# Attention, then two expert layers: another order of steps in a pair's turn, and copies dealt to other engines

## The chip, the cores and the metric

The kernel runs on one core of one Trainium2 chip. The metric is the device time of one execution in microseconds (us). The core has five engines, each with its own queue that it takes in order: TensorE (PE in the profile, its weight loads PEld), VectorE (DVE), ScalarE (ACT), GpSimd (POOL) and SyncE (SP, which here only issues transfers).

## What is computed

Causal attention with decay over 4 batches of 8 heads, 576 rows, head size 64; its output goes as 2304 rows of 512 through two expert layers of 8 experts each. The change is in the attention:

```python
scores = scale * np.matmul(q, k.transpose(0, 1, 3, 2))
cum = np.cumsum(np.log(np.clip(f, 0.0001, 1.0)), axis=-1)
decay = cum[:, :, :, None] - cum[:, :, None, :]
scores = np.where(causal, -1000000000.0, scores + decay)
attn = np.exp(scores - np.max(scores, axis=-1, keepdims=True))
attn = attn / (np.sum(attn, axis=-1, keepdims=True) + 1e-09)
out = np.matmul(attn, v)
```

The first expert layer picks one expert per row by the largest of 8 logits and weights its output with the softmax value and a second gate; the second layer gives each expert at most 288 rows in the order of the logits.

## The kernel before, in words

**Turns.** `attention` (L542) goes over 16 pairs of heads, 4 per batch, and four more turns to empty its pipeline. In turn i five generators, each a stage of another pair, are stepped one after the other; a step runs to the generator's next `yield`, and what it issues goes to the queues of its engines at once. So the order in which steps are called is the order in each engine's queue. The stages are

- **c**, `causal` (L141), for the pair of turn i+1: on POOL, the decay rows of one pair are copied with the causal mask filled in (L150, four selects of growing width, two per step), then for the last 64 rows two more selects and two copies of q into a block-diagonal tile (L156, L158). Three steps.
- **s**, `scores` (L161), for pair i: matmuls of q and k into a tile of two PSUM banks (L187; rows 0 and 1, row 2, row 3, and the tail rows, L196, whose weights are the tile that c filled), then on VectorE, per row and head, one operation that adds the mask, scales and takes the row's extreme (L176), and on ScalarE, one row later, the exponential with its sum (L173). Five steps; the last issues only the last exponential.
- **f**, `flip` (L209), for pair i-1: transposes of the exponentials on TensorE into a bank of `ps_t` (L215, L240, L245) and copies out of it into `pt` by `evac` (L203): L207 on ScalarE, L205 on VectorE, by a flag in the call. Seven steps with work: for each of the two heads j the column blocks kb=0 and kb=1 (with the last of kb=3), then kb=2 of both heads, the tail rows' four blocks (z4), and their last 64 columns.
- **v**, `values` (L250), for pair i-2: matmuls of `pt` and v into two banks, oA (columns 0 to 255) and oB (256 to 575), and copies of them into `ot`. Five steps: oA; oB for kb=0, 1, 2; oB for kb=3 and 4 with its copy.
- **r**, `rows` (L271), for pair i-3: small operations on VectorE for the reciprocal sums, then two transposes of `ot` back (L282, L288), each followed by a multiplication on VectorE out of the bank (L283, L289). Three steps with work.
- **g**, `Rt.gate` (L375), from turns 7, 11, 15 and 19 on, for a whole batch: its matmuls L381, transposes L389 and L395, a row of small operations on VectorE, the counting matmuls L421 and L424, and five scatters of rows by indirect transfers on POOL (L452), one per step. Sixteen steps, so it lasts for three turns; the last one runs by itself after the last turn.

**The order.** `ORDER` (L539) is a string written out by hand, one letter per step. After it (L589) the stages that have steps left are stepped in rounds until only g is left; so each turn has one more step of g, and the ends of c and s, behind the string. After each step of the string one small operation of the consts is issued on VectorE (`slow.issue`, L588), while there are any. At the end of a turn SP's queue gets the loads of k, q, the decay rows (cb) and, once per batch, v for the pair of two turns later (L601 to L603), and in turns 1 to 7 the clearing of a buffer (L598).

**Buffers.** PSUM has eight banks: the scores have two tiles of two, `ps_t` has two of one for all transposes of f, r and g in turn (a bank is taken again when the copy or multiplication out of it is done), oA and oB have one each. The masks of c and the tiles of f have two buffers each, loads three.

**After the attention** the last gate runs alone, the counts are ranked on VectorE, the rows are scattered and gathered by transfers, and the expert layers follow, with their weights loaded from the start of that phase.

Of the kernel before, what the change touches and what calls it, by code (L numbers as in the profile page):

```python
# [17 lines left out]
B, H, S, D = 4, 8, 576, 64  # L18
# [4 lines left out]
NQ = 4  # L23
SQ = NQ * 128
TL = S - SQ
NI = NQ + 1
T0 = 128 - TL
# [46 lines left out]
class Attention:  # L74
# [134 lines left out]
    def flip(self, zt, z4):  # L209
        nc = self.nc  # L210
        ptt = self.ptp.tile([128, 2, NQ * S + TL], F32, name="pt")
        pt = ptt[:, :, :NQ * S].rearrange("p j (k q) -> p j k q", k=NQ)

        def tr(o, z, i, kb):
            nc.tensor.transpose(o, z[:, CB0[i] + 128 * kb:CB0[i] + 128 * kb + 128], self.ident)  # L215

        for j in range(2):
            z = zt[j]
            t = self.ps_t.tile([128, 512], F32, name="tp")
            for i in range(NQ):  # L220
                tr(t[:, 128 * i:128 * i + 128], z, i, 0)
            self.evac(pt[:, j, 0, :SQ], t, j == 0)
            yield
            t = self.ps_t.tile([128, 512], F32, name="tp")
            for i in range(1, NQ):
                tr(t[:, 128 * i:128 * i + 128], z, i, 1)
            tr(t[:, 0:128], z, 3, 3)
            self.evac(pt[:, j, 1, 128:SQ], t[:, 128:SQ])
            self.evac(pt[:, j, 3, 384:SQ], t[:, 0:128])
            yield  # L230
        t = self.ps_t.tile([128, 512], F32, name="tp")
        for j in range(2):
            for i in range(2, NQ):
                o = 256 * j + 128 * (i - 2)
                tr(t[:, o:o + 128], zt[j], i, 2)
        self.evac(pt[:, :, 2, 256:SQ], t.rearrange("p (j q) -> p j q", j=2), True)
        yield
        t = self.ps_t.tile([128, 512], F32, name="tp")
        for kb in range(NQ):
            nc.tensor.transpose(t[:, 128 * kb:128 * kb + 128], z4[:, 128 * kb:128 * kb + 128], self.ident)  # L240
        self.evac(pt[:, :, :NQ, SQ:S].rearrange("p j k q -> p k j q"),
                  t.rearrange("p (k j q) -> p k j q", k=NQ, j=2))
        yield
        t = self.ps_t.tile([128, 512], F32, name="tp")
        nc.tensor.transpose(t[:, :128], z4[:, S - 128:S], self.ident)  # L245
        self.evac(ptt[T0:, :, NQ * S:], t[T0:, :128].rearrange("p (j q) -> p j q", j=2))
        yield
        return pt, ptt

    def values(self, pt, ptt, vt):  # L250
        nc = self.nc
        oA = self.ps_o.tile([128, 512], F32, name="oA")
        oB = self.ps_o.tile([128, 512], F32, name="oB")
        ot = self.op.tile([128, S], F32, name="ot")
        for t, q0, q1, kbs in ((oA, 0, 256, (0, 1)), (oB, 256, S, (0, 1, 2, 3, 4))):
            for kb in kbs:
                a = max(q0, 128 * kb)
                k0 = 0 if kb < NQ else T0
                for j in range(2):
                    nc.tensor.matmul(t[64 * j:64 * j + 64, a - q0:q1 - q0],  # L260
                                     lhsT=vt[k0:, kb, 64 * j:64 * j + 64],
                                     rhs=pt[:, j, kb, a:q1] if kb < NQ else ptt[k0:, j, NQ * S:],
                                     start=(kb == 0), stop=(kb == kbs[-1]), skip_group_check=True)
                if q0 and kb < 3:
                    yield
            self.evac(ot[:, q0:q1], t[:, :q1 - q0], q0 > 0)
            if not q0:
                yield
        return ot
# [266 lines left out]
HOLD = 6  # L536
LO = 2
LAST = "oosvsssssssssvss"
ORDER = "sfvgcfsfvgrsfvgcfsfvgrfvgr"  # L539


def attention(A, Rt, slow, weights, more, qT, kT, v):  # L542
# [10 lines left out]
    for i in range(T + 4):  # L553
# [22 lines left out]
        def step(k):  # L576
            if k in live:
                try:
                    next(live[k])
                except StopIteration as e:  # L580
                    del live[k]
                    if k != "g":
                        got[k, i - lag[k]] = e.value

        for k in ORDER:
            step(k)
# [1527 lines left out]
```

## Time and profile before

| what | value |
|---|---|
| median of 3 runs | 784.29 us (783.74 to 787.36) |
| the profiled execution's own time | 783.33 us |
| its span (first to last instruction) | 781.6 us |
| TensorE busy over the span | 707.0 us (90%) |
| VectorE, ScalarE, GpSimd busy | 370.8, 383.0, 483.0 us |
| the turns begin (first scores of turn 0) | 10.0 us |
| the experts begin (first of their transposes) | 240.6 us |

Times of rows are in microseconds from the start of the span, "mean ns" in nanoseconds. The ends of matmuls are modelled, so the distance from one group's start to the next group's start tells more than a group's length. Idle time in square brackets or behind the second bar is that of the engine just before the instruction, with what released it.

### The profile page before, as it was taken

Reading aid. Unit: us, or ns where it says so; the run is one execution under the profiler, and the core shown is the slowest. Engines: PE = TensorE matmul, PEld = TensorE weight load, DVE = VectorE, ACT = ScalarE, POOL = GpSimd, SP = SyncE. Lnnn points to the kernel's source line nnn. Section 1 sums busy time; section 2 is a strip of 40 time slices with the busy share of each in tenths; the row PEclk is TensorE's granted clock in tenths of the full one; section 3 lists DMA queues with packets and bytes.
Section 4 is the critical chain, followed back from the end, with each engine's and each line's share of the span. In section 5 each row is a group of like instructions: output and inputs, shape, how many; then the busy total and the mean of one; then the engine's idle time right before and its main releaser. Section 6 shows DMA issues by size and latency. Waiting matters only on the chain. (4 is left out here: it accounts for less than half of the span.)

```text
span 781.6 us, 16048 instructions
## 1 busy us (share of the span) xinstructions
PE 707.0 (90%) x5691; PEld 569.5 (73%) x5691; DVE 370.8 (47%) x1419; ACT 383.0 (49%) x893; POOL 483.0 (62%) x495
## 2 busy tenths in 40 slices
PE   6999999999816999999999999279999999989993
PEld 3555555555506999999999999168978878788892
DVE  4776686776752221321321323756756665651120
ACT  5777666667304454554555652134435344354440
POOL 6455318243234876777777772259868777698861
PEclk9999999999976999999999999569999999999997
DMA  6587566130138616538438430357536617366201
GB/s 215 173 290 278 167 190 216 63 121 2 42 103 279 211 52 241 184 120 273 161 138 276 156 137 12 84 166 247 193 130 206 216 47 265 113 223 200 101 33 39
DMA packets 79492, 124.33 MB, mean 159 GB/s; under 512 B 11085, under 2 KB 43853, under 8 KB 79392
## 3 DMA queue, kind: packets, MB, share of 16 engines
q1 hardware_dynamic: 73056, 104.06, 40.1%
q0 software_dynamic: 6288, 18.97, 6.7%
q8 instruction: 49, 0.80, 0.4%
q14 instruction: 51, 0.42, 0.2%
q10 hardware_dynamic: 48, 0.07, 0.0%
HBM read 101.08 MB, written 22.71 MB: 158 GB/s over the span
## 5 line engine op out<-in xcount | busy, mean ns | idle before, releaser
L699 POOL TENSOR_TENSOR wl<-wraw,wh 128x1024 fp32r<-128x1024 f32 x128 | 305.1, 2400 | 91.3 <-ACT wh L695 86.2
L729 PE MATMUL ph<-xh,wh 128*128 128x288 f32 (+6 forms) x512 | 160.8, 314 | 0.2 <-ACT xh L1922 0.2
L729 PE MATMUL ph<-xl,wh 128*128 128x288 f32 (+6 forms) x512 | 153.4, 300 | 1.5 <-DVE xl L1916 1.5
L729 PE MATMUL ph<-xh,wl 128*128 128x288 f32 (+6 forms) x512 | 153.0, 299 | 0.0
L695 ACT CAST wh<-wraw 128x1024 fp32r<-128x1024 f32 x128 | 132.0, 1050 | 42.2 <-DMA wraw<-in_moe_w_dram 42.2
L733 DVE SCALAR_TENSOR_TENSOR hl<-ph,hh 128x256 fp32r<-128x256 f32 (+6 forms) x128 | 56.3, 443 | 105.8 <-ACT hh L757 60.1
L173 ACT ACTIVATE z<-z,mx 128x128 f32<-128x128 f32 (+2 forms) x144 | 84.1, 585 | 35.4 <-DVE mx L176 34.7
L729 PEld LDWEIGHTS ph<-xh,wh 128*128 128x128 f32 x512 | 97.3, 190 | 5.2 <-issue 3.4
L757 ACT ACTIVATE hh<-ph 128x256 fp32r<-128x256 f32 (+6 forms) x128 | 51.5, 403 | 100.7 <-PE ph L729 97.1
L729 PEld LDWEIGHTS ph<-xl,wh 128*128 128x128 f32 x512 | 97.3, 190 | 2.4 <-DVE xl L1916 2.1
L729 PEld LDWEIGHTS ph<-xh,wl 128*128 128x128 f32 x512 | 97.2, 190 | 0.2 <-POOL wl L699 0.2
L176 DVE CUSTOM_DVE_ANT_0 z<-ps,cx 128x128 f32<-128x128 f32 (+2 forms) x144 | 68.9, 518 | 38.5 <-PE ps L187 23.8
L729 PE MATMUL ph<-hh,wh 128*128 128x288 f32 (+6 forms) x256 | 79.2, 309 | 0.0
L729 PE MATMUL ph<-hh,wl 128*128 128x288 f32 (+6 forms) x256 | 76.8, 300 | 0.9 <-POOL wl L699 0.8
L729 PE MATMUL ph<-hl,wh 128*128 128x288 f32 (+6 forms) x256 | 76.7, 300 | 0.0
L150 POOL TENSOR_SCALAR_AFFINE_SELECT cx<-cb 128x256 f32<-128x256 f32 (+1 forms) x64 | 44.5, 729 | 47.9 <-DMA cb<-c8d 20.3
L215 PEld LDWEIGHTS tp<-ident,z 128*128 128x128 f32 x320 | 33.6, 141 | 42.2 <-issue 12.3
L452 POOL DMA_INDIRECT xs<-x,idx x20 | 19.9, 995 | 68.2 <-DVE x L448 55.2
L215 PE MATMUL tp<-ident,z 128*128 128x128 f32 x320 | 52.2, 286 | 6.5 <-DVE pt L205 4.3
L207 ACT COPY pt<-tp 128x384 f32<-128x384 f32 (+3 forms) x112 | 43.1, 415 | 25.1 <-PE tp L245 12.4
L793 PE MATMUL ph<-wh,hh 128*128 128x512 f32 x128 | 54.2, 423 | 0.0
L793 PE MATMUL ph<-wh,hl 128*128 128x512 f32 x128 | 50.5, 394 | 0.0
(331 smaller groups left out, 1232.9 us busy)
## 6 DMA issues: line engine op xcount, KB each, us to landing
wraw<-in_moe_w_dram SPq DMA_DIRECT2D x128, 512.0 KB, 6.7
cb<-c8d SPq DMA_DIRECT2D x15, 576.0 KB, 6.1
xs<-zrow SPq DMA_DIRECT2D x8, 803.1 KB
xg<-xs SPq DMA_DIRECT2D x7, 771.0 KB, 4.8
kd<-in_k_dram SPq DMA_DIRECT2D x16, 288.0 KB, 7.7
qd<-in_q_dram SPq DMA_DIRECT2D x16, 288.0 KB, 4.7
vt<-in_v_dram SPq DMA_DIRECT2D x4, 1024.0 KB, 8.1
x<-zrow SPq DMA_DIRECT2D x1, 1080.0 KB
```

The costliest lines, as they stand in the source:

```text
L150: nc.gpsimd.affine_select(cx[:, :, CB0[i]:CB0[i] + w], cb[:, :, :w], pattern=[[0, 2], [-1, w]], compare_op=ALU.is_ge, fill=-8e9, base=128 ...
L173: nc.scalar.activation(z, z, AF.Exp, bias=mx[:, c:c + 1], scale=-1.0, accum_out=sm[:, c:c + 1])
L176: nc.vector.tensor_tensor_reduce(out=z, in0=p, in1=cx, scale=-0.125, scalar=3e38, op0=ALU.add, op1=ALU.min, accum_out=mx[:, c:c + 1])
L207: self.nc.scalar.copy(o, i)
L215: nc.tensor.transpose(o, z[:, CB0[i] + 128 * kb:CB0[i] + 128 * kb + 128], self.ident)
L452: st = nc.gpsimd.indirect_dma_start(out=self.xs[:, :], out_offset=bass.IndirectOffsetOnAxis(ap=idx[:, i:i + 1], axis=0), in_=x[:, i, :], i ...
L695: nc.scalar.copy(wh, t)
L699: nc.gpsimd.tensor_sub(wl[:, q], t[:, q], wh.bitcast(F32)[:, q])
L729: mm = lambda o, w, m, st, sp: nc.tensor.matmul(o, lhsT=w, rhs=m, start=st, stop=sp)
L733: nc.vector.scalar_tensor_tensor(out=hl[:, :W], in0=p[:, :W], scalar=0.0, in1=hh.bitcast(F32)[:, :W], op0=ALU.max, op1=ALU.subtract)
L757: nc.scalar.activation(hh[:, :W], p[:, :W], AF.Relu)
L793: mm = lambda o, w, m, st, sp: nc.tensor.matmul(o, lhsT=w, rhs=m, start=st, stop=sp)
```

## The change

The copies' engines come from a table (1 is VectorE, 0 ScalarE), and the string of steps is another one. In the old calls the flag was true (VectorE) for kb=0 of j=0, for kb=2 and for oB. No operation is added or removed; the string has 27 steps in place of 26, the new one being the fifth of s.

```diff
@@ flip
-            self.evac(pt[:, j, 0, :SQ], t, j == 0)
+            self.evac(pt[:, j, 0, :SQ], t, EVAC[j][0])
...
-            self.evac(pt[:, j, 1, 128:SQ], t[:, 128:SQ])
-            self.evac(pt[:, j, 3, 384:SQ], t[:, 0:128])
+            self.evac(pt[:, j, 1, 128:SQ], t[:, 128:SQ], EVAC[j][1])
+            self.evac(pt[:, j, 3, 384:SQ], t[:, 0:128], EVAC[j][2])
...
-        self.evac(pt[:, :, 2, 256:SQ], t.rearrange("p (j q) -> p j q", j=2), True)
+        self.evac(pt[:, :, 2, 256:SQ], t.rearrange("p (j q) -> p j q", j=2), EVAC[2])
...
         self.evac(pt[:, :, :NQ, SQ:S].rearrange("p j k q -> p k j q"),
-                  t.rearrange("p (k j q) -> p k j q", k=NQ, j=2))
+                  t.rearrange("p (k j q) -> p k j q", k=NQ, j=2), EVAC[3])
...
-        self.evac(ptt[T0:, :, NQ * S:], t[T0:, :128].rearrange("p (j q) -> p j q", j=2))
+        self.evac(ptt[T0:, :, NQ * S:], t[T0:, :128].rearrange("p (j q) -> p j q", j=2), EVAC[4])
@@ values
-            self.evac(ot[:, q0:q1], t[:, :q1 - q0], q0 > 0)
+            self.evac(ot[:, q0:q1], t[:, :q1 - q0], EVAC[5][q0 > 0])
@@
-ORDER = "sfvgcfsfvgrsfvgcfsfvgrfvgr"
+EVAC = [(0, 0, 0), (1, 0, 0), 0, 1, 1, (0, 0)]
+ORDER = "vgvffsvvgfrfgsrfscvrfsfggsc"
```

## Rows read from the trace of the kernel before

**Rows 1.** The page, its first line.
```profile
span 781.6 us, 16048 instructions
```

**Rows 2.** Stretches: length, then each engine's busy time; turns 5, 7 and 8.
```profile
60.83:72.50 11.67, 11.67 (x80) 6.51 (x79) 7.99 (x29) 8.35 (x27) 8.37 (x15) 1.00 0.70 243
84.16:98.54 14.38, 13.92 (x101) 7.39 (x100) 8.86 (x31) 9.15 (x29) 3.30 (x7) 1.00 0.45 139
98.54:111.70 13.16, 12.32 (x99) 7.07 (x98) 12.02 (x50) 8.46 (x29) 0.72 (x1) 1.00 0.57 172
```

**Rows 3.** Timeline of TensorE in turn 5: start, length, instruction.
```profile
60.83 0.93 PE L187 MATMUL ps<-kd,qd 64*128 64x128 f32 x8
61.69 0.66 PE L215 MATMUL tp<-ident,z 128*128 128x128 f32 x4
62.27 0.87 PE L260 MATMUL oA<-pt,vt 128*64 128x256 f32 x8
63.08 0.66 PE L215 MATMUL tp<-ident,z 128*128 128x128 f32 x4
63.66 0.92 PE L187 MATMUL ps<-kd,qd 64*128 64x384 f32 x4
64.51 0.66 PE L215 MATMUL tp<-ident,z 128*128 128x128 f32 x4
65.10 0.76 PE L260 MATMUL oB<-pt,vt 128*64 128x320 f32 x4
65.78 1.13 PE L187 MATMUL ps<-kd,qd 64*128 64x512 f32 x4
...
68.12 0.66 PE L215 MATMUL tp<-ident,z 128*128 128x128 f32 x4
68.61 1.14 PE L196 MATMUL ps<-kd,tail 128*128 128x288 f32 x4
```

**Rows 4.** Timeline of TensorE where groups of one shape are neighbours, turns 1 and 17.
```profile
17.41 1.09 PE L215 MATMUL tp<-ident,z 128*128 128x128 f32 x8
18.43 0.92 PE L187 MATMUL ps<-kd,qd 64*128 64x384 f32 x4
...
211.16 1.78 PE L260 MATMUL oB<-pt,vt 128*64 128x320 f32 x12
212.87 0.66 PE L282 MATMUL tp<-ident,ot 128*128 128x128 f32 x4
```

**Rows 5.** Timeline of turn 3, the instructions that waited.
```profile
36.21 0.93 PE L187 MATMUL ps<-kd,qd 64*128 64x128 f32 x8 [0.86 <-DMA qd<-in_q_dram]
...
37.73 2.77 POOL L150 TENSOR_SCALAR_AFFINE_SELECT cx<-cb 128x256 f32<-128x256 f32 x4 [8.88 <-DMA cb<-c8d]
...
38.17 0.29 DVE L176 CUSTOM_DVE_ANT_0 z<-ps,cx 128x128 f32<-128x128 f32 x1 [1.90 <-POOL cx L150]
...
41.18 0.66 PE L215 MATMUL tp<-ident,z 128*128 128x128 f32 x4 [1.23 <-DVE pt L205]
```

**Rows 6.** Groups by shape, 20 to 215 us: busy, mean ns, idle before.
```profile
L207 ACT COPY pt<-tp 128x512 f32<-128x512 f32 x32 | 18.5, 577 | 9.9 <-PE tp L240 9.2 <-PE tp L215 0.7
...
L207 ACT COPY ot<-oA 128x256 f32<-128x256 f32 x16 | 6.0, 373 | 2.8 <-PE oA L260 2.6
...
L205 DVE COPY pt<-tp 128x512 f32<-128x512 f32 x31 | 21.3, 688 | 4.9 <-PE tp L215 4.6
```

**Rows 7.** Timeline of VectorE in turn 5, the copy right behind four score rows.
```profile
63.06 0.69 DVE L205 COPY pt<-tp 128x512 f32<-128x512 f32 x1
```

**Rows 8.** Timeline of turn 8's end: the tail scores, and POOL's scatters with what follows.
```profile
107.82 1.14 PE L196 MATMUL ps<-kd,tail 128*128 128x288 f32 x4
...
110.98 1.19 POOL L452 DMA_INDIRECT xs<-x,idx  x1 [15.00 <-DVE x L448]
...
112.48 0.97 POOL L452 DMA_INDIRECT xs<-x,idx  x1 [0.21 <-issue]
...
117.24 0.67 POOL L156 TENSOR_SCALAR_AFFINE_SELECT cx<-cb 64x576 f32<-64x576 f32 x1 [2.92 <-DMA xs<-x,idx]
```

**Rows 9.** Timeline: TensorE's first work for the experts.
```profile
240.64 2.79 PE L716 MATMUL tq<-ident,xg 128*128 128x128 f32 x12 [17.09 <-DMA xg<-xs]
```

## Prediction, made before the changed kernel was run

> **What bounds the kernel now.** I read the page first: the span is 781.6 us [rows 1], beside 783.33 us for the same execution's own time; the median of the runs shown is 784.29, so the sum below stands on an execution 0.96 us faster than the median. Then the view by stretches, cut at the start of each pair's turn. A plain turn with all of s, f, v, r and c lasts 11.67 us, and TensorE is busy for all 11.67 of it, ScalarE for 8.35, VectorE for 7.99 [rows 2]. Turns that also carry a gate last 14.38 and 13.16 us, with TensorE idle for 0.46 and 0.84 of that [rows 2]. So in the steady state nobody keeps TensorE waiting: its own instruction stream is the turn, and an order that leaves its time alone cannot gain.
>
> The list of TensorE in a plain turn shows where its time can shrink [rows 3]. Each group of matmuls has an array shape: 64\*128 for scores, 128\*128 for transposes, 128\*64 for the value matmuls. Four transposes take 0.58 us from their start to the next group's when that has another shape (61.69 to 62.27), but 0.49 when it has the same (68.12 to 68.61). The group after a change of shape also starts slowly: eight transposes in a row, two groups joined, take 1.02 us (17.41 to 18.43), against 2 x 0.585 apart, and the three value groups at 211.16, which follow another value group, take 1.71 against 3 x 0.68 apart [rows 3, 4]. A **boundary** between shapes thus costs about 0.15 us, 0.09 behind the last matmul and 0.06 ahead of the next. (The Trainium skill, TensorE: Matmul & The Clock Gate, The mechanism, says that weight loads overlap running matmuls only where the row group differs, which would leave the 0.06 standing in joined groups; it is weighed below.)
>
> Around turn 3 the trace shows another limit: TensorE starts it 0.86 us late for a load of q, VectorE waits 1.90 for a mask that POOL could start only after the decay rows landed (8.88 idle), and a copy behind that on VectorE holds TensorE 1.23 at 41.18 [rows 5].
>
> **The change part by part.** *Order.* By shape the old turn is s | f | v | f | s | f | v | s | f | v | f s f | v | r f | v | r: 15 boundaries, counting the one to the next turn. The new one is v v | f f | s | v v | f f | s | r f | s | v | r f s f: 10. Work is equal, so a plain turn loses 5 x 0.15 = 0.75 us: 10.92, if the two banks of the transposes keep up.
>
> They should. New turn, from its start: v v 0.81 + 0.68 - 0.15 = 1.34; f f to 2.36; s to 3.22; v v to 4.44; f f to 5.46; s to 6.31 [rows 3, 4]. The first pair of copies (ScalarE) has some 2 us until f's banks are wanted again at 4.44. The tightest is the third f's copy, now on VectorE: its matmuls end 0.66 after 4.44, the copy takes 0.69 [rows 3, 6], so it is done near 5.8; r wants the bank at 6.31. Ahead of it on VectorE are the four score rows, which in the old turn are done 2.23 us after the scores' start (60.83 to 63.06) [rows 3, 7], here at 4.6. **Margin 0.5 us.** Queued behind the copy are r's small operations and the next rows, which the same margin covers.
>
> *Copies.* The two j=0/j=1 copies swap engines. The kb=2 copy of 512 moves to ScalarE and that of z4 to VectorE: equal counts, 0.577 on ScalarE against 0.688 on VectorE [rows 6]. oB (320 wide) moves to ScalarE, bounded by its 256 and 512 wide copies, 0.373 and 0.577, and a 64x128 one goes the other way, bounded by 0 and 0.373 [rows 6]. ScalarE gets 0 to 0.6 us more, I take 0.2: 8.55 busy in 10.92, hidden behind TensorE; VectorE gets less. Without that cover each 0.1 would be 1.3 us over 13 turns.
>
> *s first becomes s sixth.* Scores start 2.36 us into the turn. At turn 3 this hides the late q (0.86) and the late mask (1.90), and with it the 1.23. With four boundaries fewer in turn 2, which has no r (0.6), and turn 3's own 0.75, turns 2 and 3 could give 0.86 + 1.23 + 0.6 + 0.75 = 3.4; turn 1 gains no boundary, and its first f now waits for the exponentials of turn 0, so I take **3.0**. The loads on SP's queue are issued at the end of a turn as before.
>
> *Gate turns.* The gate's matmuls fall so that boundaries lost and added by them are equal; of the idle 0.46 and 0.84 I take back 0.1 and 0.3: 0.85 and 1.05 (bounds: none or all of it).
>
> *c later, and the extra steps.* POOL takes its queue in order. In the old turn c's four wide selects precede the gate's scatter; now the second c (two selects, about two thirds of 2.77) stands behind the first scatter, and the rest of c behind the second. In turn 8 the old scatter starts at 110.98, 3.16 us after the tail scores (107.82) [rows 8]. The new tail scores start 1.2 before the turn's end, with a short copy (under 0.4) more ahead, so the scatter starts about 2.4 into turn 9. Adding 1.2 for it, 1.8 for the selects and 0.3, the second is issued at 5.7. A select of the rest of c waits for its landing: 112.48 to 117.24, 4.76 us [rows 8]; so 10.5, and with that select and the copy behind it about 11.4, later if a landing takes longer. The tail scores want that copy at 9.75. **A new wait of about 2.0 us** (bounds 0 and 2.8) on TensorE in turns 9 and 13; turn 17 has no scores. What is behind it there: f's last transpose and the next turn's v.
>
> *End of attention.* Turn 16 (f, v, r, gate) loses 5 boundaries, 0.75, and some bank waits; I take 1.3. From there to the first matmul of the experts everything hangs in one chain: TensorE waits 17.09 us for the gathered rows [rows 9], and before those come the last gate and its scatters. So the experts shift whole.
>
> *Sum:* turns 2 and 3, 3.0; plain turns 4, 5, 6, 9, 10, 13, 14: 7 x 0.75 = 5.25; gate turns 7, 11, 15: 3 x 0.85 = 2.55, and 8, 12: 2 x 1.05 = 2.1; end 1.3: 14.2. Minus 2 x 2.0 = 4.0 for POOL's wait: **10.2 us less**, 773.1 on this execution, and 773.6 allowing half of its distance to the median.
>
> **The rivals.**
> *POOL's wait is not there* (the select's wait is of something else, or the scatter starts sooner): 14.2 less, 769.6. For it: the profile only infers who released the select; against: the wait returns at each batch. 0.14.
>
> *Bank waits eat half:* two joined f's fill both banks at once, and margins are about 0.5 us. If 0.4 a turn is lost, 13 x 0.4 = 5.2: 778.8. For it: VectorE has 12.02 us of work in 13.16 in the second gate turn [rows 2]; against: plain turns leave 3 us of VectorE free. 0.14.
>
> *Slower:* the third f's copy, behind four score rows on VectorE, holds r, and so all of TensorE behind it. It decides from a copy 0.5 + 0.75 = 1.25 us later than worked out, in every turn. At 1.75 later the turn is 10.92 + 1.25 = 12.17: 14.2 - 4.0 - 13 x 1.25 = 6 us slower, 789.9. For it: at 41.18 exactly this wait stands, from 1.9 us of lateness [rows 5]; against: that had a load as its cause, and plain turns show none. 0.05.
>
> *Joined transposes keep their slow start,* so a boundary saves 0.09 only: 0.3 less in each of some 14 turns, 4.2 in all: 777.8. The trace speaks against it, with 1.02 for eight transposes [rows 4]. (This is the rule of the Trainium skill, TensorE: Matmul & The Clock Gate, The mechanism; by it the sum would be 6.0 instead of 10.2, and the trace does not agree with it.) 0.02.
>
> *It does nothing:* if the 0.15 belonged to waiting for a bank, not to the shape, a group that waits would keep it; turn 3's 2.1 would be gained and 4.0 given back: 785, give or take 2. Against: the tail scores wait for a bank too and start without the gap [rows 3]. 0.05.
>
> **How the numbers follow.** The forecast gets 0.60. Its own range, from the bounds of POOL's wait, the gate turns and the start, is 770 to 777. The range reaches to the two cases of 0.14: 768 to 780. Under 0.5% (3.9 us), about what a measurement of this kernel can tell from no change, lie the idle case and a small part of the half-eaten one: 0.08. Slower by more: 0.05. Faster: 0.87.
>
> **What would show it.** Right: plain turns of 10.9 us with TensorE still busy throughout; eight transposes and two value groups in a row at their joined lengths; turn 3's waits gone; in turns 9 and 13 the tail scores waiting on POOL's copy; the experts' first matmul some 10 us earlier with the same distance to the last gate. Wrong: TensorE's waits for copies or for VectorE's multiplications inside plain turns; turns at 11.6; the experts not moving with the attention.

## The result, and the profile after

The changed kernel takes **774.11 us** (median of 4 runs, 773.05 to 776.86), the kernel before 784.16 (4 runs, 783.74 to 787.36): a ratio of 0.9871, 95% interval 0.9851 to 0.989. The forecast was 773.6, with a range of 768 to 780. The profiled execution is the slowest of the four, 776.86, and beside [rows 1] the first line of its page reads:

```profile
span 775.1 us, 16037 instructions
```

So the two profiles differ by 6.5 us where the medians differ by 10.05. Of the four runs of the changed kernel the slower ones have the lower mean granted clock (0.953, 0.954, 0.957 and 0.958, from 776.86 down to 773.05). Where the rest went is in the table at the end of this section.

**The turns.** A turn now begins with oA. Stretches of the changed kernel cut there, columns as in [rows 2]: a plain turn (6), the two gate turns (7, 8), and turns 9 and 13.

```profile
69.08:80.00 10.92, 10.92 (x80) 6.60 (x79) 7.89 (x29) 8.55 (x27) 5.72 (x14) 1.00 0.82 289
80.00:93.69 13.69, 13.44 (x101) 7.42 (x100) 8.69 (x31) 9.39 (x30) 4.52 (x10) 1.00 0.54 173
93.69:105.82 12.13, 11.60 (x100) 7.07 (x99) 11.24 (x46) 8.29 (x27) 0.00 (x0) 1.00 0.62 190
105.82:118.22 12.40, 11.18 (x79) 6.62 (x79) 8.69 (x33) 8.61 (x28) 6.89 (x12) 1.00 0.39 140
155.67:166.83 11.16, 11.16 (x80) 6.62 (x79) 8.55 (x33) 8.65 (x28) 6.69 (x12) 1.00 0.46 154
```

Against 11.67, 14.38 and 13.16 in [rows 2], a plain turn lost 0.75, the gate turns 0.69 and 1.03. TensorE is still busy for all of a plain turn, and ScalarE for 8.55 us. The list of TensorE in turn 6 shows the joins, to be laid beside [rows 3, 4]:

```profile
69.08 0.87 PE L260 MATMUL oA<-pt,vt 128*64 128x256 f32 x8
69.78 0.71 PE L260 MATMUL oB<-pt,vt 128*64 128x320 f32 x4
70.42 1.09 PE L215 MATMUL tp<-ident,z 128*128 128x128 f32 x8
71.45 0.93 PE L187 MATMUL ps<-kd,qd 64*128 64x128 f32 x8
72.30 1.30 PE L260 MATMUL oB<-pt,vt 128*64 128x320 f32 x8
73.53 1.09 PE L215 MATMUL tp<-ident,z 128*128 128x128 f32 x8
74.55 0.92 PE L187 MATMUL ps<-kd,qd 64*128 64x384 f32 x4
75.40 0.66 PE L282 MATMUL tp<-ident,ot 128*128 128x128 f32 x4
```

From the turn's start, the ends of the joined groups lie at 1.34, 2.37, 3.22, 4.45, 5.47 and 6.32; the prediction had 1.34, 2.36, 3.22, 4.44, 5.46 and 6.31. Eight transposes take 1.02 us (73.53 to 74.55) and not 2 x 0.585. The copy with the tightest margin, on VectorE, starts in time:

```profile
74.22 0.69 DVE L205 COPY pt<-tp 128x512 f32<-128x512 f32 x1 [0.47 <-PE tp L215]
```

It ends at 74.91, 5.83 into the turn, and the transposes of r that take its bank start at 75.40: a margin of 0.49 us.

**Turn 3.** The waits of [rows 5] for q, for the mask and for the copy behind it are gone. POOL's selects start no earlier, since the decay rows land as late as before, but the scores come later than both:

```profile
38.25 2.76 POOL L150 TENSOR_SCALAR_AFFINE_SELECT cx<-cb 128x256 f32<-128x256 f32 x4 [8.97 <-DMA cb<-c8d]
...
38.43 0.93 PE L187 MATMUL ps<-kd,qd 64*128 64x128 f32 x8
...
39.54 0.29 DVE L176 CUSTOM_DVE_ANT_0 z<-ps,cx 128x128 f32<-128x128 f32 x1 [1.50 <-PE ps L187]
```

**The new wait.** POOL's queue at the end of turn 9 with the tail scores on TensorE, and in turn 13 the second scatter with the select behind it:

```profile
108.25 1.19 POOL L452 DMA_INDIRECT xs<-x,idx  x1 [14.79 <-DVE x L448]
...
111.51 0.99 POOL L452 DMA_INDIRECT xs<-x,idx  x1 [0.19 <-issue]
...
116.03 0.66 POOL L156 TENSOR_SCALAR_AFFINE_SELECT cx<-cb 64x576 f32<-64x576 f32 x1 [2.66 <-DMA xs<-x,idx]
116.65 0.24 POOL L158 COPY tail<-qd 64x64 f32<-64x64 f32 x1
...
116.94 1.24 PE L196 MATMUL ps<-kd,tail 128*128 128x288 f32 x4 [1.23 <-POOL tail L158]
...
161.13 0.99 POOL L452 DMA_INDIRECT xs<-x,idx  x1 [0.17 <-issue]
...
164.64 0.66 POOL L156 TENSOR_SCALAR_AFFINE_SELECT cx<-cb 64x576 f32<-64x576 f32 x1 [1.64 <-DMA xs<-x,idx]
```

The scatters of turn 9 are issued 2.43 and 5.69 us into it (worked out: 2.4 and 5.7), and 4.52 us pass from the second issue to the select that waits for the landing (4.76 in [rows 8]; that it waits for the landing is inferred by the profile). The tail scores wait 1.23 us for POOL's copy. In turn 13 the landing took 3.51, and the profile shows no wait; but the tail scores start right behind POOL's copy there, 0.58 us behind the start of the group before them instead of 0.43 in a plain turn, and the turn is 0.25 longer. The view of waits gives what is left of TensorE's waits, here without those ahead of turn 0 and in the counts of the gates:

```profile
PE ps L196 <- POOL tail L158: 1.4, 2, 1.2
PE tp L381 <- DVE x L283: 1.3, 1, 1.3
PE tp L215 <- DVE carry L435: 1.1, 2, 0.5
PE tp L389 <- DVE pt L205: 0.6, 3, 0.2
PE tp L288 <- ACT pt L207: 0.2, 1, 0.2
```

Columns: us in total, times, longest. Of the first row 0.2 is turn 0's, and the second row is the last gate's. Only the last row is a bank wait in a plain turn (turn 5, 11.19 us).

**The end.** The last gate's first matmuls before and after, and the experts' first transposes after (240.64 before):

```profile
216.94 1.18 PE L381 MATMUL tp<-ot,wgb 128*32 128x288 f32 x16 [1.43 <-DVE x L283]
...
206.66 1.97 PE L381 MATMUL tp<-ot,wgb 128*32 128x288 f32 x16 [1.30 <-DVE x L283]
...
231.49 2.79 PE L719 MATMUL tq<-ident,xg 128*128 128x128 f32 x12 [17.21 <-DMA xg<-xs]
```

The last gate comes 10.28 us earlier, the experts 9.15, the end of the span 6.5. The loss on the way is the clock, in nearly all of it. In the profile after, the granted clock falls to 0.50 at 206.9, within the last gate: from the start of its 16 matmuls to the transposes behind them 1.90 us pass instead of 1.21, and those transposes take 1.05 instead of 0.76. That is 0.98 of the 1.13 lost there. In the experts, the stretch between the two layers, before and after, and a second one after:

```profile
489.10:519.80 30.70, 11.60 (x166) 8.61 (x165) 20.41 (x95) 3.67 (x6) 11.95 (x12) 0.50 0.37 110
...
480.00:514.10 34.10, 16.64 (x188) 13.47 (x184) 20.88 (x97) 4.76 (x11) 10.86 (x10) 0.50 0.45 143
684.80:691.60 6.80, 6.07 (x26) 6.10 (x27) 2.23 (x5) 2.00 (x4) 5.67 (x7) 0.50 0.58 195
```

Before, the clock was at 1.00 from the first of these stretches to 772.4, so the second has no counterpart. Laid side by side matmul by matmul, the two traces show what each is worth. The experts begin at the half clock in both, but until 2.7 us after their first transposes in the profile after and until 6.1 before, and by then the lead has grown from 9.15 to 10.8. Behind the first stretch it is 9.1, behind the second 6.5, and between these places it does not change by more than 0.2.

Where the time went, stage by stage, in two pairs of profiles (positive is gained). The second pair comes from the experiments (experiment 9), which ran on other chips, on which the kernel before takes about 800 us:

| stage | predicted | this pair | the other pair |
|---|---|---|---|
| up to the start of turn 2 | -0.4 | -1.43 | 0.30 |
| turns 2 and 3 | 3.4 | 3.61 | 3.76 |
| turns 4 to 16 without POOL's wait (from experiment 3) | 11.2 | 10.70 | 10.68 |
| POOL's wait (2.08 of the 2.71) and other losses, turns 4 to 16 | -4.0 | -2.71 | -2.01 |
| turn 17 up to the last gate | 0 | 0.11 | 2.60 |
| last gate to the experts | 0 | -1.13 | -0.63 |
| experts to the end | 0 | -2.65 | -0.90 |
| sum, spans | 10.2 | 6.5 | 13.8 |

### The profile page after: what moved, and what is told of

It reads as the page before. It is cut to its first block, busy times and chain, and to the rows that moved or that the text cites. A ratio compares the mean times of both kernels' runs of the same rounds, so it can differ in the third digit from the quotient of the medians.

```text
span 775.1 us, 16037 instructions
## 1 busy us (share of the span) xinstructions
PE 704.7 (91%) x5691; PEld 576.0 (74%) x5691; DVE 368.4 (48%) x1419; ACT 383.3 (49%) x893; POOL 482.8 (62%) x495
## 5 line engine op out<-in xcount | busy, mean ns | idle before, releaser
L796 PE MATMUL ph<-wl,hh 128*128 128x512 f32 x128 | 50.3, 393 | 0.0
L187 PE MATMUL ps<-kd,qd 64*128 64x128 f32 (+3 forms) x256 | 49.6, 488 | 0.1
L732 PEld LDWEIGHTS ph<-hh,wl 128*128 128x128 f32 x256 | 48.3, 189 | 1.4 <-POOL wl L702 1.4
```

The costliest lines, as they stand in the source:

```text
L187: nc.tensor.matmul(p[:, j, o:o + w], lhsT=qd[h, 128 * i:128 * i + 128], rhs=kd[h, :w], start=True, stop=True, skip_group_check=True)
L732: mm = lambda o, w, m, st, sp: nc.tensor.matmul(o, lhsT=w, rhs=m, start=st, stop=sp)
L796: mm = lambda o, w, m, st, sp: nc.tensor.matmul(o, lhsT=w, rhs=m, start=st, stop=sp)
```

## The experiments

My theory: the boundaries between array shapes cost TensorE 0.15 us each, so the string of steps sets the turn, as long as the two banks of the transposes keep up; the copies only serve that. The rivals: the copies bring the gain; the gain is turn 3's; or bank waits decide and not the boundaries. All ratios below are to the kernel before, run beside each on the same chip.

**1. The order alone.**

```diff
-EVAC = [(0, 0, 0), (1, 0, 0), 0, 1, 1, (0, 0)]
+EVAC = [(1, 0, 0), (0, 0, 0), 1, 0, 0, (0, 1)]
```

> The new string of steps with the copies on their old engines. If the gain is that of boundaries between array shapes (15 in a plain turn before, 10 after, 0.15 us each), a plain turn stays at 10.9 to 11.2 us and the time within 3 us of the changed kernel's 774. If the gain needs the copies dealt anew, because the transposes' two banks come free too late otherwise, plain turns last 11.4 us or more, with TensorE waiting for VectorE's copies, and the time is 780 or more.

783.79 us, ratio 0.9808 (0.9791 to 0.9824): the whole gain. A plain turn and a first gate turn of it:

```profile
69.01:80.04 11.03, 11.03 (x80) 6.60 (x79) 8.24 (x29) 8.45 (x27) 6.16 (x15) 1.00 0.92 303
80.04:93.46 13.42, 13.33 (x101) 7.35 (x100) 8.39 (x30) 9.36 (x29) 4.47 (x10) 1.00 0.59 183
```

The new copies are worth 0.11 us in a plain turn and 0.53 in a second gate turn (12.66 here), and cost 0.27 in a first one, where the gate's transposes (L389) wait 0.2 for the copy that moved to VectorE. Over turns 4 to 16 that is 152.12 against 150.60 us in the second run of experiment 3, 1.5 us, and the runs don't show it: beside the kernel before, the changed kernel has ratios of 0.9824 and 0.983 on such chips (experiment 9), no lower than this one.

**2. The copies alone.**

```diff
-ORDER = "vgvffsvvgfrfgsrfscvrfsfggsc"
+ORDER = "sfvgcfsfvgrsfvgcfsfvgrfvgr"
```

> The old string of steps with the copies on their new engines: 15 boundaries again. By the boundaries a plain turn lasts 11.67 us or a little more, the waits of turn 3 are back, and the time is 784 (782 to 788). If the copies carry a part of the gain by themselves, the time is 780 or less.

801.14 us, ratio 1.0021 (1.0006 to 1.0035): nothing gained. Plain turns take 11.74 us, and new bank waits appear in the view of waits:

```profile
PE tp L215 <- ACT pt L207: 4.3, 8, 0.9
```

So the deal of the copies gains nothing in the old order. The waits of turn 3 did not come back as expected: it began at 37.32, later than before, the view lists no wait for q in it, and it lasted 11.74.

**3. c's two wide selects ahead of the scatters**, tried twice.

```diff
-ORDER = "vgvffsvvgfrfgsrfscvrfsfggsc"
+ORDER = "vgvffsvvgfrfgsrfscvrfscfggs"
```

> The changed kernel with the last step of c moved ahead of the two last steps of the gate. If the tail scores of turn 9 wait 1.2 us because two selects stand behind the first scatter on POOL, and the second scatter behind them, that wait goes or shrinks under 0.3 and the time falls by about 1 us. If the wait comes from the scatters' landing alone, whatever stands ahead of them, it stays at 1.2 and the time does not move.

> The changed kernel with all of c's last steps put ahead of the gate's scatters in the same string. Theory (the wait for POOL costs 1.2 to 1.5 us in turn 9 and 0 to 1.5 in turn 13): turn 9 at 10.91 again, no wait of the tail scores for POOL in either turn, and 1 to 2.5 us less than the changed kernel of this call, ratio to it 0.997 to 0.999. Rival (the wait is covered, as the time that TensorE loses there only moves the wait of the chain behind the last gate): the same time within 0.5 us.

783.08 us, ratio 0.9803 (0.9787 to 0.9819), and again 783.47, 0.9788 (0.9764 to 0.9813). The changed kernel beside the second run takes 786.27, ratio 0.983 (0.9803 to 0.9856), so the medians put this string, c first for short, 2.8 us ahead of the change; the runs of the two overlap (782.01 to 785.42 and 784.45 to 788.37). The traces show where it gains. Turn 9 of the changed kernel beside it, and then turn 9 with c first:

```profile
104.43:116.81 12.38, 11.18 (x80) 6.62 (x79) 8.69 (x33) 8.60 (x28) 6.88 (x12) 1.00 0.39 140
```

```profile
105.50:116.42 10.92, 10.92 (x80) 6.60 (x79) 8.39 (x33) 8.41 (x27) 5.16 (x10) 1.00 0.44 159
```

Turn 13 goes from 11.45 to 10.91, and turns 4 to 16 from 152.61 to 150.60 in all. The wait of the tail scores is gone in both traces with c first, but not as the expectation of the second run says: what moved ahead of the scatters is c's second step, the two wide selects. c's last step, the selects and copies for the tail rows, still stands behind the second scatter and still waits for its landing:

```profile
109.44 0.97 POOL L452 DMA_INDIRECT xs<-x,idx  x1 [0.21 <-issue]
...
114.08 0.67 POOL L156 TENSOR_SCALAR_AFFINE_SELECT cx<-cb 64x576 f32<-64x576 f32 x1 [2.80 <-DMA xs<-x,idx]
```

That is 4.64 us, no less than in the changed kernel. But without the wide selects (1.84 us) between the scatters the second one is issued 3.94 us into the turn instead of 5.69, and the copy for the tail is done 0.3 ahead of the tail scores. So the wait comes from the place of the wide selects together with the landing, and c first hides the landing rather than removing it.

**4. Two joins undone.**

```diff
-ORDER = "vgvffsvvgfrfgsrfscvrfsfggsc"
+ORDER = "vgfvfsvgfvrfgsrfscvrfsfggsc"
```

> The changed kernel with the two pairs of v and f taken apart (v f v f in place of v v f f, twice): scores still come late, copies stay, banks have more room, but a plain turn has 14 boundaries in place of 10. By the boundaries a plain turn lasts 10.92 + 4 x 0.15 = 11.5 us and the time is about 782. If the gain is that of the late scores, or of room in the banks, plain turns stay at 10.9 and the time at 774.

788.34 us, ratio 0.9872 (0.9855 to 0.9889). Four boundaries more than the changed kernel, 14 in all, should give 10.91 + 4 x 0.15 = 11.51. A plain turn and a first gate turn:

```profile
58.58:70.09 11.51, 11.51 (x79) 6.44 (x79) 8.18 (x29) 8.39 (x27) 6.53 (x14) 1.00 0.77 279
81.60:95.19 13.59, 13.53 (x101) 7.35 (x100) 8.71 (x31) 9.27 (x30) 4.52 (x10) 1.00 0.52 167
```

The plain turns 4 to 6 and 9 take 11.51 to 11.52. The gate turns did not get longer (13.59 against 13.69): in the changed string the gate's matmuls stand inside the joined groups and split them, here they stand where a boundary is anyway.

**5. The scores first again, with ten boundaries.**

```diff
-ORDER = "vgvffsvvgfrfgsrfscvrfsfggsc"
+ORDER = "sgvvffsgrrfsgcvrfsfggvvffsc"
```

> The same ten boundaries as the changed kernel, but the scores start the turn (s, v v, f f, s, r f, s, v, r f s f, v v, f f). If boundaries set the plain turn, it lasts 10.9 us plus what the banks' waits cost in this order; if late scores are what spared turn 3 its waits, turn 3 starts late or waits for q, the mask and a copy again, 1 to 2 us in all, so that the time is 1 to 2 us over the changed kernel's. If late scores do not matter, turn 3 is like the others.

800.68 us, ratio 1.0001 (0.9986 to 1.0017): the same number of boundaries, and all of the gain lost. Plain turns take 11.70 at best. One of them, and the longest group of waits:

```profile
49.21:60.91 11.70, 11.34 (x79) 6.57 (x78) 7.57 (x28) 8.18 (x27) 4.65 (x10) 1.00 0.83 285
```

```profile
PE tp L215 <- DVE pt L205: 1.9, 7, 0.3
```

So the count of boundaries sets a floor that a string need not reach. Of the 0.79 us over 10.91, TensorE stands idle for 0.36, and waits for banks are what the view lists; for the rest it counts as busy, and that this too comes of the banks, which two neighbouring steps use too close together, is argued and not shown. What late scores are worth in turn 3 this run does not tell: its turn 3 began at 37.47, 1.3 later than before, and found q there.

**6 and 7. More value steps joined:** eight and nine boundaries.

```diff
-ORDER = "vgvffsvvgfrfgsrfscvrfsfggsc"
+ORDER = "vvvvvgffsgfrfgsrfscrfscfggs"
```

> All five steps of v in a row at the turn's start, c ahead of the gate's last steps: 8 boundaries. By the boundaries alone a plain turn lasts 10.92 - 0.3 = 10.6 us and the time falls 4 us under the changed kernel with c first. If the copies now set the pace (the third f's copy on VectorE comes 0.2 us late for r's bank by my working), it is 10.8 or more and the time within 2 us of it.

```diff
-ORDER = "vgvffsvvgfrfgsrfscvrfsfggsc"
+ORDER = "vvvvgffsgfrfgsvrfscrfscfggs"
```

> Four steps of v in a row, the fifth between the second scores and r, c ahead of the gate's last steps: 9 boundaries. By the boundaries alone a plain turn lasts 10.92 - 0.15 = 10.77 us. If the copies set the pace it stays at 10.9 or above, with TensorE waiting for ScalarE's copy ahead of z4's transposes.

794.43 us, ratio 0.9945 (0.9922 to 0.9968), and 794.33, 0.9933 (0.991 to 0.9955). By the count alone the plain turns would be 10.91 - 0.30 = 10.61 and 10.76. A plain turn of the first, and its longest group of waits:

```profile
69.95:81.41 11.46, 10.75 (x80) 6.76 (x79) 7.48 (x29) 8.29 (x27) 5.26 (x13) 1.00 0.81 262
```

```profile
PE tp L288 <- ACT pt L207: 6.7, 10, 1.5
```

TensorE has less to do (10.75 instead of 10.92) and waits 0.71 for a bank: with all of v at the front, f and r come too close together behind it. In experiment 7 the plain turns take 11.16 at best, and the waits there are for VectorE's multiplications (L283), not for ScalarE's copy as expected. The gate turns lose more each: 14.80 and 12.97 in experiment 6, 14.96 and 13.05 in experiment 7, against 13.70 and 12.13 with c first. Ten boundaries is the best of the counts tried: neither of the two strings with fewer came without waits for banks.

**8. The gate's steps later.** With c first as well.

```diff
-ORDER = "vgvffsvvgfrfgsrfscvrfscfggs"
+ORDER = "vgvffsvvfrfsgrfgscvrfscfggs"
```

> The string with c first, and the gate's second step moved behind the second scores and its third behind the fifth f. Theory (in turns 8 and 12 TensorE waits some 0.5 us for VectorE's carry, with work behind it that could go ahead): turns 8 and 12 go from 12.1 to 11.6, turns 7, 11 and 15 stay within 0.3 of 13.7, and the sum is 1 us less than with c first alone. Rival (the boundaries that the gate's matmuls add in their new place, 0.15 each, or waits for VectorE's multiplications, take it back): turns 8 and 12 at 12.1 to 12.5, and 0 to 2 us more than with c first alone.

786.91 us, ratio 0.9849 (0.9819 to 0.9879): 3.4 us more than with c first alone, where 1 us less was expected. The gate turns grew to 14.14 and 12.81:

```profile
78.88:93.02 14.14, 13.29 (x100) 7.44 (x99) 8.70 (x31) 9.39 (x30) 4.75 (x10) 1.00 0.59 189
93.02:105.83 12.81, 11.61 (x100) 7.08 (x99) 11.21 (x46) 8.45 (x27) 1.55 (x3) 1.00 0.61 180
```

```profile
PE tp L215 <- DVE carry L435: 3.1, 3, 1.2
PE tp L215 <- ACT us L383: 2.6, 3, 1.1
```

The wait for VectorE's carry did not go, it doubled from 0.5 to 1.2, and one for ScalarE's copy of the gate (L383) came with it: f, behind the gate in the string, waits for the bank that the gate has taken. That the gate's later place brings f closer behind it is argued from the string, not tried by itself.

**9. The changed kernel and the kernel before, unchanged,** for their profiles on these chips.

> The changed kernel as it is, beside the others on one chip. Its plain turns should last 10.91 us again and its ratio to the kernel before be within its first interval, 0.985 to 0.989. The order alone came out at 0.981 on another chip, where the kernel before took 799.8 us: if that ratio is the chip's and not the copies' doing, this one comes out near 0.981 there too.

> The changed kernel, unchanged, beside the two variants of this call. Theory: ratio 0.982 to 0.988 to the kernel before, plain turns 10.91, and turns 9 and 13 again longer than a plain turn by 0 to 1.5 us through the wait of the tail scores for POOL's copy. Rival (that wait came by chance in the two profiles): turns 9 and 13 of 10.91 here.

> The kernel before, unchanged, for its profile on the same chip as the next three. Theory (the order saves TensorE's time per boundary between array shapes, so the saving doesn't depend on the chip): plain turns of 11.67 us within 0.05 and the last gate some 10.3 us behind that of the changed kernel, and what these chips add to the time (about 800 instead of 784 us) lies mostly behind the attention, in the expert layers. Rival (the larger gain of 14 us on these chips is one of the attention): the attention of this profile is longer than the first one's by 3 us or more, in turns with transfers (2, 3 and the gate turns), with plain turns at 11.67.

The changed kernel: 786.19 us, ratio 0.9824 (0.9796 to 0.9852), and 786.27, 0.983 (0.9803 to 0.9856), both below the first chip's 0.985 to 0.989. Its plain turns 4 to 6 are 10.91 to 10.96 in both. Turn 9 waits 1.47 and 1.20 for POOL, turn 13 nothing and 0.26, so the wait is no accident of one profile, but its size varies. In the first of the two the granted clock was 0.50 from 116.4 to 119.8, right behind that wait of 1.47, and turns 9 and 10 took 13.40 and 11.80. The kernel before: one run, 798.33 us, with plain turns of 11.67:

```profile
49.94:61.61 11.67, 11.67 (x81) 6.51 (x80) 7.87 (x29) 8.36 (x27) 4.83 (x10) 1.00 0.83 278
```

So the saving per turn is that of the first chip. The last gate lies 15.3 us behind that of the changed kernel, not 10.3 as expected. By the table, the larger difference of this pair (13.8 us in the spans) lies at the ends of the attention and in the experts: 0.30 instead of -1.43 up to turn 2, 2.60 instead of 0.11 from turn 17 to the last gate, where a stall held the kernel before, and -0.90 instead of -2.65 in the experts. That is one pair of profiles; whether these differences hold for all runs and explain the larger gain in the medians (14 us) is not shown.

## Why the prediction was right, and where it was not

- **A boundary costs 0.15 us: right, and shown.** Ten, fourteen and fifteen boundaries gave 10.91, 11.51 and 11.67 us where no bank was waited for, and the ends of the groups inside the turn fell within 0.01 of those worked out. It was right because both parts, 0.09 behind and 0.06 ahead, were read from pairs of neighbours that the old kernel already had [rows 3, 4]. (The Trainium skill, TensorEngine Tiling (Array Packing), Key Properties: "Changing tiling mode (not just tile) drains the TensorE". The trace agrees, with these 0.15 us as the price.)
- **"Joined transposes keep their slow start": refuted.** Eight take 1.02 and 1.03 us in turn 6, where two f's are joined. (The Trainium skill, TensorE: Matmul & The Clock Gate, The mechanism, has weight loads overlap running matmuls only where the row group differs, though the same section also names a background weight buffer; the same group of rows is loaded eight times here, and the trace does not agree with the first.)
- **"Bank waits eat half": not in this string.** One plain turn of seven loses 0.28 us (turn 5). Experiments 5 to 7 show that this was a matter of the string: with other strings more than half of the gain is lost, or all of it. The tightest margin was put at 0.5 us and measured 0.49.
- **The copies cost nothing: right in a plain turn.** ScalarE was put at 8.55 and has 8.55 in turn 6.
- **Turns 2 and 3: right by size, wrong where it ends.** The 3.4 was 3.61 and 3.76, the smaller part of the gain, so the rival that the gain is turn 3's falls. "Turn 1 gains no boundary, and its first f now waits", for which 0.4 was taken off, came to 1.43 in the first pair and to a gain of 0.30 in the other. The clock makes about 1.1 of this difference of 1.73: the trace after has no record of the full clock until 19.2 us (14.6 before, 15.3 for the changed kernel of the other pair; the view of stretches prints 1.00 where there is no record), and eight transposes at 17.65 took 1.71 us instead of 1.02 [rows 4]. The other 0.6 is the kernel before, which came to turn 2 that much later on the second chip.

```profile
17.65 1.78 PE L215 MATMUL tp<-ident,z 128*128 128x128 f32 x8
19.36 0.93 PE L187 MATMUL ps<-kd,qd 64*128 64x128 f32 x8
```

- **Gate turns: 0.85 was 0.69; 1.05 was 1.03.** The step "boundaries lost and added by the gate's matmuls are equal" fails in the first gate turn: TensorE's busy time there fell by 0.48 (13.92 to 13.44) and not by 0.75. By the string, L381 stands between two joined value groups and splits them, and in experiment 4 undoing the joins cost that turn no time. To this comes the wait of 0.2 for the copy that moved to VectorE (experiment 1).
- **POOL's wait: right in place and cause, mis-sized.** It was put at 2 x 2.0. With c first (experiment 3) turns 9 and 13 get back 1.47 and 0.54 us on the same chip, 2.0 in sum; in the first profile turns 9, 10 and 13 are 1.48, 0.35 and 0.25 longer than a plain turn, 2.08 in sum, where the tail scores start behind POOL's copy. Two steps failed. The prediction's own times, 11.4 for the copy and 9.75 for the tail scores, give 1.65, and 2.0 was taken with no row for the rest. And the landing of one scatter, 4.76, was taken for all: it was 4.52, 4.76 and 4.50 in turn 9 of three profiles of the changed kernel, but 3.51, 3.31 and 3.78 in turn 13, and in experiment 1 short enough for no wait:

```profile
111.25 0.99 POOL L452 DMA_INDIRECT xs<-x,idx  x1
...
114.48 0.67 POOL L156 TENSOR_SCALAR_AFFINE_SELECT cx<-cb 64x576 f32<-64x576 f32 x1 [1.36 <-DMA xs<-x,idx]
```

That is 3.23 us. What sets it stays open. As an estimate, turn 9 of the changed kernel grows as soon as the landing takes longer than about 3.0 us (4.52 made it 1.48 longer), and turn 13, where the second scatter is issued 0.23 us earlier, as soon as it takes longer than 3.3 (3.51 made it 0.25 longer).

- **"The experts shift whole": not in the profile.** The lead was 10.28 at the last gate and 6.5 at the end of the span, for the clock's reasons above. The median of the runs gives 10.05, the forecast was 10.2. That they agree this closely is in part luck: the clock, which the forecast left out, and POOL's wait, which it over-priced by some 2 us, lie on opposite sides, and the median run is less disturbed by the clock than the profiled one.

The best string found is c first: 783.47 against 786.27 us for the change and 800.56 for the kernel before, on one chip.

## What to carry to other kernels

When TensorE is busy for the whole of a turn, look at the array shapes of neighbouring groups before looking for waits: each change of shape cost 0.15 us here, and steps of several stages can be reordered to lie together. The count of changes is a floor only; write down for each bank when its copy is done and when the next group wants it, because with margins under half a microsecond the same count gave a turn of 10.91 or 11.70. And when a step stands behind a transfer on an in-order queue, price it with several landings of that transfer and with the time at which the transfer is issued: landings of 3.2 and 4.8 us were the difference between no wait and one of 1.5, and with the transfer issued 1.75 us earlier in the turn a landing of 4.6 cost nothing.

## What was not expected of the hardware

- The clock differs between runs of one kernel. In the two profiles of c first the record of the full clock begins at 13.3 and 19.4 us, and turn 2 at 24.42 and 25.65; the half-clock stretch between the expert layers lasted 34.1 us in one and 30.7 in the other.
- In eight of the twelve profiles from the chips of the experiments one engine stands still for 1.6 us or more near the end of the attention, and the profile names no releaser on the core. In the kernel before it hits VectorE ahead of the copy of oB, and the last gate waits for it:

```profile
217.59 0.49 DVE L205 COPY ot<-oB 128x320 f32<-128x320 f32 x1 [2.17 <-remote]
```

In the changed kernel, where ScalarE copies oB, it hits ScalarE in the last gate:

```profile
207.85 0.40 ACT L383 COPY us<-tp 128x288 f32<-128x288 f32 x1 [1.83 <-remote]
```

Neither of the two profiles of the first chip has it. What it is stays open.
